# Local value products as four matmuls with a head's high and low parts side by side, and a slot's work in another order

## The chip, the cores and the metric

The kernel runs on one core of one Trainium2 chip. The metric is the device time of one execution in microseconds; the time before is the median of three runs. The engines are TensorE (PE in the profile, its weight loads PEld), VectorE (DVE), ScalarE (ACT), GpSimd (POOL) and SyncE (SP), whose queue starts the transfers.

## What is computed

Attention with a window and a few global tokens, for 8 batches of 8 heads, and behind it a feed-forward layer on all tokens. Sl is 512, Sg is 32, D is 64; the layer has d_model 512 and d_ff 2048. Cut to what matters:

```python
def _attn_ref(q_l, k_l, v_l, q_g, k_g, v_g):
    window, scale = 32, 1.0 / np.sqrt(D)
    k_all = np.concatenate([k_g, k_l], axis=2)
    v_all = np.concatenate([v_g, v_l], axis=2)
    out_g = sm(scale * q_g @ k_all.T) @ v_all            # global queries see all keys
    s_ll = np.where(np.abs(i - j) <= window, scale * q_l @ k_l.T, -1e9)
    s_lg = scale * q_l @ k_g.T                           # local queries: window and global keys
    out_l = sm(np.concatenate([s_lg, s_ll], -1)) @ np.concatenate([v_g, v_l], axis=2)
    return np.concatenate([out_g, out_l], axis=2)

def _moe_ref(x, w_in, w_out):
    h = np.maximum(x @ w_in, 0.0)
    return h * h @ w_out
```

## The kernel before

**Slots.** Batch, half of the sequence and head give 8 x 2 x 8 = 128 attention units of 256 queries. One loop runs over slots t. In slot t the scores and the softmax of unit t are computed, the probabilities of unit t-1 are transposed, split and multiplied by the values, and the inputs of unit t+1 are split. The same slot runs step m = t - 9 of the feed-forward layer: `gemm1` (two halves j of 12 products into `h`), `act1` and `act2` (relu, square, split into `gh` and `gl`), and `gemm2` of step m-1 (12 products into the two `o` tiles). Eight units make one group of 256 rows, and eight steps one block of the layer, so a block's output is copied out (`evac`, tile `ot`) every eighth slot, at t = 2 and 10 of 16. The global queries' own work is a list of jobs spread over slots; it repeats every 16 slots, which is one batch. Below, "slot 14" means t = 14 modulo 16.

**Split operands.** Units before t = 16 are plain: they use float32 products. From t = 16 on an operand is split in two parts of the type fp32r, a high part that is the rounded copy (made by ACT) and a low part that is the remainder (made by DVE, original minus high). A product is then high by high, high by low and low by high. `hi` holds a unit's keys (352 columns), queries (256) and values (256) in one tile, `lo` the remainders of the queries and of three quarters of the values; the keys' remainders lie in the lower 64 partitions of `hi`. `pt` (PSUM) holds the transposed probabilities, `ph` and `pl` their parts. `xa` (PSUM) is the attention output of a unit, transposed; `x_evac` splits it into `x_h` and `x_l`, the inputs of `gemm1`.

**Value products before.** `av` runs nine matmuls with weights of 64 columns (a value block, high or low) into the same 64 partitions of `xa`: for each half of the queries three with 128 columns, two more with 128 for the middle block, one with 256 for the global values, whose parts lie stacked.

**Buffers.** PSUM is full: two tiles `h`, two `o`, and one each of `pt`, `s`, `xa` and `gs`. The buffer of `xa` is shared with `gt` (the transposed global probabilities) and `gxo` (their products with the values), so each of these starts only when the last read of the one before is done. Global jobs that matter here, with their slots: `g_soft` and `g_exp` (2, 12), `g_norm` and `g_tr` with `gt` (3, 13), `g_rest` (`ptl`, `pth`) and the split of the first pair's values `gvh`, `gvl` (4, 14), `g_av` with `gxo` (4, 7, 14, 1), the split of the second pair's values (6, 0), `g_x` (5, 8, 15, 2).

**Order.** From t = 17 on every instruction of PE, DVE and ACT goes into its engine's queue in the order in which the program is written; `InOrder` sees to that, and it is why most lines of the profile carry the line of that helper (L52). Before that a scheduler chooses. A job's second number in the list is its place in the slot: 5 ahead of the scores, 4 ahead of the softmax, 3 behind it, 2 ahead of `gemm2`, 0 and 1 at the end.

Of the kernel before, what the change touches and what calls it, by code (L numbers as in the profile page):

```python
# [16 lines left out]
P = 128  # L17
# [9 lines left out]
LAG = 9  # L27
# [4 lines left out]
LOOK = 2  # L32
SQ = (2, 3, 4, 5, 14, 15)
MUL = 9
# [3 lines left out]
def f(ap):  # L38
    return ap.bitcast(F32)
# [19 lines left out]
def attention_moe(  # L59
# [22 lines left out]
    def plain(t):  # L82
        return t < NPLAIN
# [3 lines left out]
    def w_take(n):  # L87
        w_bufs["free"] -= n
# [35 lines left out]

    def split_head(t):

        hd = heads[t]
        raw = hd["raw"]
        if plain(t):
            return  # L130
        hi = p2.tile([P, PK], F32R, tag="hi", name=f"hi{t}")
        lo = p2.tile([P, QC + 192], F32R, tag="lo", name=f"lo{t}")
        ac.copy(hi, raw)
        ve.tensor_sub(lo, raw[:, KC : KC + QC + 192], f(hi[:, KC : KC + QC + 192]))
        ve.tensor_sub(hi[64:, :KC], raw[64:, :KC], f(hi[64:, :KC]))
        ve.tensor_sub(hi[32:64, PK - 64 :], raw[32:64, PK - 64 :], f(hi[32:64, PK - 64 :]))
        hd["hi"], hd["lo"] = hi, lo

# [45 lines left out]

    def softmax3(t):
        st = heads[t]["st"]
        pr = prob[t % 2]
        ve.tensor_scalar(out=st[:, 6:8], in0=st[:, 4:6], scalar1=1e-9, scalar2=None, op0=ALU.add)
        ve.reciprocal(out=st[:, 0:2], in_=st[:, 6:8])
        for u in range(2):  # L190
# [11 lines left out]
    def pt_split(t):  # L202
        hd = heads[t]
        if plain(t):
            pts = p2.tile([P, 512], F32, tag="gh", name=f"pts{t}")
            ac.copy(pts, pt)
            hd["pts"] = pts
            return
        ph = p1.tile([P, 640], F32R, tag="ph", name=f"ph{t}")
        pl = p1.tile([P, 256], F32R, tag="pl", name=f"pl{t}")  # L210
# [4 lines left out]
        hd["ph"], hd["pl"] = ph, pl  # L215

    def pt_rest(t):
        if plain(t):
            return
        ph, pl = heads[t]["ph"], heads[t]["pl"]  # L220
        ve.tensor_sub(pl, pt[:, :256], f(ph[:, :256]))
        ve.tensor_sub(ph[64:, 256:384], pt[:64, 320:448], f(ph[:64, 256:384]))

        ve.tensor_sub(ph[64:, 384:640], pt[64:, 256:512], f(ph[:64, 384:640]))

    def av(t):
        hd = heads[t]
        c = QC + KC
        if plain(t):

            xa = ps_a.tile([P, HALF], F32, tag="xa", name=f"xa{t}")
            v, pts = hd["raw"][:, c:], hd["pts"]
            mm = [
                (xa, v[:, 0:128], pts[:, 256:512]),
                (xa[:, 0:128], v[:, 64:192], pts[:, 0:128]),
                (xa[:, 128:256], v[:, 128:256], pts[:, 128:256]),
            ]
        else:
            xa = ps_a.tile([64, HALF], F32, tag="xa", name=f"xa{t}")
            vh, vl, ph, pl = hd["hi"][:, c:], hd["lo"][:, QC:], hd["ph"], hd["pl"]  # L240
            mm = []
            for u in range(2):
                o, vs, ps = xa[:, 128 * u : 128 * u + 128], slice(64 * u, 64 * u + 64), slice(128 * u, 128 * u + 128)
                mm += [(o, vh[:, vs], ph[:, ps]), (o, vl[:, vs], ph[:, ps]), (o, vh[:, vs], pl[:, ps])]
            o = xa[:, 64:192]
            mm += [(o, vh[:, 128:192], ph[:, 256:384]), (o, vl[:, 128:192], ph[:, 256:384])]
            mm.append((xa, vh[:, 192:256], ph[:, 384:640]))
        for i, (o, a, b) in enumerate(mm):
            pe.matmul(o, a, b, start=i == 0, stop=i == len(mm) - 1, skip_group_check=True)
        hd["xa"] = xa[:64, :]  # L250

    def x_evac(t):
        g, h = divmod(t, 8)
        xa = heads[t]["xa"]
        r = slice((h % 2) * 64, (h % 2) * 64 + 64)
        if g == 0:
            ac.copy(xg[r, h // 2, :], xa)
        else:
            ac.copy(x_h[r, g % 2, h // 2, :], xa)
            ve.tensor_sub(x_l[r, g % 2, h // 2, :], xa, f(x_h[r, g % 2, h // 2, :]))  # L260
        heads[t] = None
# [180 lines left out]

    def gemm1(m, j):
# [145 lines left out]
    for t in range(NSTEP + LAG + 1):  # L589
# [181 lines left out]
```

## Time and profile before

| | |
|---|---|
| median of the runs | 1068.83 us (1068.39 to 1069.07) |
| the profiled execution | 1068.82 us, span 1067.0 us |
| PE busy, matmuls | 1050.4 us (98%), 7568 |
| PEld busy | 941.7 us (88%) |
| DVE busy | 856.3 us (80%), 2687 instructions |
| ACT busy | 753.1 us (71%), 1901 instructions |
| granted TensorE clock | 1.00 |
| transfers | 96.78 MB, mean 91 GB/s |

Matmuls overlap, so PE's busy time is nearly the span and says little by itself. The chain of work that ended last tells more: followed back from the last instruction, it names at each step what released the next one. A group's line gives busy time and mean ns of one behind the bar, and behind a second bar the idle time of the engine just before it and what ended most of that. In the lines names stand without buffer numbers, output first: `xa<-ph,hi` is a product into xa.

### The profile page before, as it was taken

The page shows a single profiled execution, that of the slowest core. Times are in us where ns is not written, and L with a number is a line of the kernel's source. Part 1 is how long each engine was busy: PE and PEld are TensorE (multiplying, and loading weights), DVE is VectorE, ACT ScalarE, POOL GpSimd, SP SyncE. Part 2 cuts the span into 40 slices and gives each one's busy share as a digit, 9 for nine tenths or more (in the row PEclk, how much of TensorE's full clock was granted, in tenths as well). Part 3 has the DMA queues.
Part 4 walks back from the last instruction along what each step waited for, and adds up shares of the span by engine and source line. Part 5 has one row for each costly group of instructions (what it writes and reads, how often), then busy time and mean ns, then how long its engine had stood idle before and what let it go on. Part 6 is the DMA issues. An engine that isn't in the chain of part 4 may idle for free.

```text
span 1067.0 us, 21142 instructions
## 1 busy us (share of the span) xinstructions
PE 1050.4 (98%) x7568; PEld 941.7 (88%) x7568; DVE 856.3 (80%) x2687; ACT 753.1 (71%) x1901; POOL 3.9 (0%) x14
## 2 busy tenths in 40 slices
PE   7999999999999999999999999999999999999998
PEld 6776889999998989998999989999999989999896
DVE  5698988898888989988888888888888888874321
ACT  5898877778777776778777777777777787774322
POOL 1000000000000000000000000000000000000000
PEclk9999999999999999999999999999999999999999
DMA  9772132223222322222322222223221322201000
GB/s 372 310 263 74 57 106 76 71 80 98 68 89 64 103 65 83 74 91 77 94 71 82 86 72 76 90 66 100 78 89 55 94 86 66 88 29 33 13 20 20
DMA packets 54312, 96.78 MB, mean 91 GB/s; under 512 B 4288, under 2 KB 29376, under 8 KB 54208
## 3 DMA queue, kind: packets, MB, share of 16 engines
q1 hardware_dynamic: 54064, 95.37, 27.2%
q8 instruction: 60, 0.98, 0.4%
q14 instruction: 44, 0.36, 0.1%
q10 hardware_dynamic: 144, 0.07, 0.0%
HBM read 86.51 MB, written 8.91 MB: 89 GB/s over the span
## 4 chain that ended last, share of the span: by engine, by line
PE 87%; ACT 7%; DVE 4%; issue 1%; DMA 0%; ACTq 0%
PE o L52 33%; PE h L52 32%; PE xa L52 7%; PE s L52 6%; PE pt L52 5%; PE gxo L52 2%; PE gs L52 2%; ACT prob L52 1%; DVE prob L52 1%; ACT r L52 1%; ACT ph L52 1%; ACT hi L52 1%; ACT ot L52 1%; PE gt L52 1%; ACT sg L52 0%
## 5 line engine op out<-in xcount | busy, mean ns | idle before, releaser
L52 PE MATMUL h<-x_h,ws 128*128 128x256 f32 x2048 | 388.9, 283 | 0.0
L52 PEld LDWEIGHTS h<-x_h,ws 128*128 128x128 f32 x2048 | 327.0, 191 | 0.5
L52 PE MATMUL o<-ws,gh 128*128 128x512 f32 x1024 | 321.3, 395 | 0.0
L52 PE MATMUL h<-x_l,ws 128*128 128x256 f32 x1024 | 289.1, 282 | 0.1
L52 PEld LDWEIGHTS o<-ws,gh 128*128 128x128 f32 x1024 | 185.5, 188 | 34.6
L52 PE MATMUL o<-ws,gl 128*128 128x512 f32 x512 | 202.6, 396 | 0.0
L52 PEld LDWEIGHTS h<-x_l,ws 128*128 128x128 f32 x1024 | 195.9, 191 | 0.9 <-DVE x_l L52 0.4
L52 ACT CAST ph<-pt 128x256 fp32r<-128x256 f32 x448 | 141.1, 341 | 67.7 <-PE pt L52 60.8
L52 ACT ACTIVATE prob<-prob,st 128x224 f32<-128x224 f32 x270 | 127.8, 475 | 61.2 <-DVE st L52 59.1
L52 ACT ACTIVATE r<-h 128x512 f32<-128x512 f32 x136 | 81.4, 599 | 112.3 <-PE h L52 112.3
L52 PEld LDWEIGHTS o<-ws,gl 128*128 128x128 f32 x512 | 96.2, 188 | 22.7
L52 DVE CUSTOM_DVE_ANT_0 prob<-s,con 128x224 f32<-128x224 f32 x256 | 90.0, 386 | 24.5 <-PE s L52 23.2
L52 DVE TENSOR_TENSOR gl<-r,gh 128x512 fp32r<-128x512 f32 x128 | 87.9, 686 | 23.3 <-ACT gh L52 20.5
L52 ACT CAST hi<-raw 128x864 fp32r<-128x864 f32 x112 | 102.5, 915 | 1.4
L52 DVE TENSOR_TENSOR r<-h,r 128x512 f32<-128x512 f32 x82 | 56.7, 692 | 51.9 <-ACT r L52 50.6
L52 PE MATMUL xa<-ph,hi 128*64 128x128 f32 x448 | 87.3, 238 | 1.6 <-DVE ph L52 1.2
L52 DVE TENSOR_TENSOR hi<-raw,hi 64x352 fp32r<-64x352 f32 x224 | 82.5, 368 | 6.4
L52 ACT CAST gh<-r 128x512 fp32r<-128x512 f32 x128 | 79.1, 618 | 9.1 <-DVE r L52 8.7
L52 DVE TENSOR_TENSOR ph<-pt,ph 64x128 fp32r<-64x128 f32 x224 | 79.6, 355 | 7.0
L52 DVE TENSOR_TENSOR lo<-raw,hi 128x448 fp32r<-128x448 f32 x112 | 69.6, 622 | 15.3 <-ACT hi L52 12.5
L52 PE MATMUL pt<-con,prob 128*128 128x128 f32 (+1 forms) x512 | 78.2, 274 | 0.7 <-ACT prob L52 0.5
L52 DVE TENSOR_SCALAR prob<-prob,st 128x224 f32<-128x224 f32 x242 | 70.7, 334 | 4.1
(80 smaller groups left out, 1572.7 us busy)
## 6 DMA issues: line engine op xcount, KB each, us to landing
raw<-in_pk_dram SPq DMA_DIRECT2D x127, 432.0 KB, 3.2
wr<-in_w_dram SPq DMA_DIRECT2D x32, 512.0 KB, 7.9
gv<-in_vg_dram SPq DMA_DIRECT2D x32, 320.0 KB, 3.3
out_dram<-ot SPq DMA_DIRECT2D x32, 256.0 KB, 2.2
qr<-in_qg_dram SPq DMA_DIRECT2D x31, 64.0 KB, 2.8
out_dram<-ot SPq DMA_DIRECT2D x8, 64.0 KB, 1.7
con<-in_consts_dram SPq DMA_DIRECT2D x2, 224.0 KB, 5.1
raw<-in_pk_dram SPq DMA_DIRECT2D x1, 304.0 KB, 3.2
```

The source lines that it names most:

```text
L52: r = method(*args, **kwargs)
```

## The change

Four parts of one edit.

- **Values apart.** `split_head` becomes `split_kq` and `rest_kq` (keys and queries, tile `kq`, 608 columns copied by ACT, two remainders by DVE) and `split_v` (tile `v`, high and low part of each value block side by side in 128 columns). From t = 17 on `split_kq` and `rest_kq` of unit t+1 stand around the softmax of unit t; `split_v` stays late in the slot.
- **Four products.** The probabilities' parts lie side by side too (`ps`). A matmul has weights of 128 columns, the high and the low part of a value block, so `xa` has 128 partitions: high by high and high by low of the values come out one below the other, and the products with the low part of the probabilities in columns next to them. Four matmuls move 128, 256, 256 and 256 columns; the first two write their output in two pieces with a gap between. `x_evac` then adds up the parts: after the copy to `x_h` three operations on DVE that read `xa`, through a new tile `xr`, in place of one.
- **Order.** The remainders of the probabilities (`pt_rest`) go ahead of the softmax; `g_scores` and the value products go between the two halves of `gemm1`'s second part; `x_evac` goes ahead of `act1`; the scaling of the second half of the probabilities moves from DVE to ACT, behind the square.
- **Square.** It is on ACT in every slot up to t = 127, before in 6 of 16 slots (and on DVE in the others); behind that it is on DVE. The first output tile of a block takes the buffer of `pth` instead of one of its own. The host stacks the global values twice, 64 partitions apart, where it did three times, 32 apart.

```diff
-SQ = (2, 3, 4, 5, 14, 15)
...
+    def split_kq(t):
...
+        raw, c = hd["raw"], QC + KC
+        kq = p2.tile([P, c + QC], F32R, tag="kq", name=f"kq{t}")
+        ac.copy(kq[:, :c], raw[:, :c])
+        hd["hi"], hd["lo"] = kq[:, :c], kq[:, c:]
+
+    def rest_kq(t):
...
+        ve.tensor_sub(hd["lo"], raw[:, KC : KC + QC], f(hi[:, KC:]))
         ve.tensor_sub(hi[64:, :KC], raw[64:, :KC], f(hi[64:, :KC]))
-        ve.tensor_sub(hi[32:64, PK - 64 :], raw[32:64, PK - 64 :], f(hi[32:64, PK - 64 :]))
+
+    def split_v(t):
...
+        ac.copy(vs[:, :, :64], vr)
+        ve.tensor_sub(vs[:, :, 64:], vr, f(vs[:, :, :64]))
...
-            if MUL <= t < NPLAIN:
+            if MUL <= t < NPLAIN or t >= NPLAIN and u == 1:
                 ac.activation(out=w_, in_=w_, func=AF.Copy, scale=st[:, u : u + 1])
...
-        ac.copy(ph[:, :256], pt[:, :256])
-        ac.copy(ph[:64, 256:384], pt[:64, 320:448])
-        for r in (0, 32):
-            ac.copy(ph[r : r + 32, 384:640], pt[64:96, 256:512])
+        ac.copy(pb[:, :, 0, :], pt[:, :256].rearrange("p (u n) -> p u n", u=2))
+        ac.copy(ps[:64, 512:640], pt[:64, 320:448])
+        ac.copy(ps[:64, 640:], pt[64:, 256:])
...
+            xa = ps_a.tile([P, 512], F32, tag="xa", name=f"xa{t}")
+            xb = xa.rearrange("p (u h n) -> p u h n", u=2, h=2)
+            ps, vs = hd["ps"], [hd["v"][:, 128 * i : 128 * i + 128] for i in range(4)]
+            both = bass.AP(xa.tensor, xa.offset + 64, [list(xa.ap[0]), [192, 2], [1, 64]])
+            mm = [(both, vs[2], ps[:, 512:640]), (xb[:, :, 0, :], vs[3], ps[:, 640:])]
+            mm += [(xa[:, 256 * u : 256 * u + 256], vs[u], ps[:, 256 * u : 256 * u + 256]) for u in range(2)]
...
+            ac.copy(x0, xb[:64, :, 0, :])
+            ve.tensor_sub(xr, xb[:64, :, 0, :], f(x0))
+            ve.tensor_add(xr, xb[:64, :, 1, :], xr)
+            ve.tensor_add(x1, xb[64:, :, 0, :], xr)
...
-        if m < 8 or m + LAG < NT + 8 and (m + LAG) % 16 in SQ:
+        if m + LAG < NT:
             ac.activation(out=r, in_=r, func=AF.Square)
...
+        late, split = prev and not plain(t - 1), t + 1 < NT
         if prev:
             pt_split(t - 1)
+            if late:
+                pt_rest(t - 1)
...
+        if split and late:
+            split_kq(t + 1)
         if live:
             softmax1(t)
             softmax2(t)
-        if prev:
-            pt_rest(t - 1)
+        if split and late:
+            rest_kq(t + 1)
...
-            gemm1(m, 1)
+            gemm1(m, 1, 0 if late else None)
+        if live and not early:
+            g_scores(t)
         if prev:
             av(t - 1)
-        if live and not early:
-            g_scores(t)
+        if run and late:
+            gemm1(m, 1, 1)
...
         if live and not early:
-            softmax3(t)
+            softmax3(t, (0,))
+        if late:
+            x_evac(t - 1)
         if run:
             act1(m)
+        if live and not early:
+            softmax3(t, (1,))
```

How the queues read, on DVE in slot 14 before, from the softmax on: ISA and the row behind it are the masked maximum of one half of the scores `s`, `st` holds a row's maximum and sum, `prob` the probabilities; the rows with `gv` are the split of the global values.

```order
L52 ISA prob_93,st_2468<-s_2440,con 128x224
L52 ISA st_2468 128x1
...
L52 TENSOR_SCALAR st_2468<-st_2468 128x2
L52 TENSOR_TENSOR pl_2459<-pt,ph_2458 128x256
L52 TENSOR_TENSOR ph_2458<-pt,ph_2458 64x128
L52 TENSOR_TENSOR ph_2458<-pt,ph_2458 64x256
L52 TENSOR_TENSOR gvl_0_2478<-gv_0_2208,gvh_0_2477 128x512
L52 TENSOR_TENSOR gvh_0_2477<-gv_0_2208,gvh_0_2477 32x128
...
L52 RECIPROCAL st_2468<-st_2468 128x2
L52 TENSOR_SCALAR prob_93<-prob_93,st_2468 128x224 x2
L52 TENSOR_TENSOR x_l<-xa_2494,x_h 64x256
```

The probabilities' remainders stand behind the softmax, and one row reads xa.

The same slot on DVE now, from the remainders on (`ph` is the tile `ps` of the code):

```order
L51 TENSOR_TENSOR ph_2421<-pt,ph_2421 128x2x128
L51 TENSOR_TENSOR ph_2421<-pt,ph_2421 64x128
L51 TENSOR_TENSOR ph_2421<-pt,ph_2421 64x256
L51 TENSOR_TENSOR ptl_2428<-gt_2389,pth_2394 128x512
...
L51 ISA prob_93,st_2434<-s_2403,con 128x224
...
L51 TENSOR_TENSOR kq_2432<-raw_2290,kq_2432 128x256
...
L51 TENSOR_TENSOR gvl_0_2443<-gv_0_2177,gvh_0_2442 128x512
...
L51 TENSOR_SCALAR prob_93<-prob_93,st_2434 128x224
L51 TENSOR_TENSOR xr_2469<-xa_2455,x_h 64x256
L51 TENSOR_TENSOR xr_2469<-xa_2455,xr_2469 64x256
L51 TENSOR_TENSOR x_l<-xa_2455,xr_2469 64x256
```

The remainders stand ahead of the softmax, those of k and q between it and the global values, and three rows read xa.

On ACT in the same slot before, from the copies of `pt` on:

```order
L52 CAST ph_2458<-pt 32x256 x2
L52 CAST pth_2431<-gs_2290 64x128
L52 ACTIVATE prob_93,st_2468<-prob_93,st_2468 128x224 x2
L52 CAST gvh_0_2477<-gv_0_2208 128x640
L52 ACTIVATE r_2510<-h_2445 128x512
L52 ACTIVATE r_2510<-r_2510 128x512
L52 CAST x_h<-xa_2494 64x256
L52 CAST hi_2515<-raw_2324 128x864
L52 CAST gh_2535<-r_2510 128x512
```

And on ACT now:

```order
L51 CAST ph_2421<-pt 64x256
L51 CAST pth_2394<-gs_2245 64x128
L51 CAST kq_2432<-raw_2290 128x608
L51 ACTIVATE prob_93,st_2434<-prob_93,st_2434 128x224 x2
L51 CAST gvh_0_2442<-gv_0_2177 128x640
L51 CAST x_h<-xa_2455 64x256
L51 ACTIVATE r_2474<-h_2408 128x512
L51 ACTIVATE r_2474<-r_2474 128x512
L51 ACTIVATE prob_93<-prob_93,st_2434 128x224
L51 CAST v_2478<-raw_2290 128x4x64
L51 CAST gh_2495<-r_2474 128x512
```

The copy of keys and queries stands ahead of the exponentials (the row with x2), the copy of the values late; x_h has moved ahead of r, and a scaling of prob stands behind the square.

On PE around the value products, before:

```order
L52 MATMUL h_2445<-x_h,ws_994 128x256
L52 MATMUL xa_2494<-ph_2458,hi_2301 64x128
L52 MATMUL xa_2494<-ph_2458,lo_2302 64x128
L52 MATMUL xa_2494<-pl_2459,hi_2301 64x128
...
L52 MATMUL xa_2494<-ph_2458,hi_2301 64x256
L52 MATMUL gs_2504<-hi_2400,qgz 128x288
L52 MATMUL o_2_2105<-ws_961,gh_2422 128x512 x2
```

And now:

```order
L51 MATMUL h_2408<-x_h,ws_992 128x256
L51 MATMUL gs_2453<-kq_2321,qgz 128x288
L51 MATMUL xa_2455<-ph_2421,v_2270 128x2x64
L51 MATMUL xa_2455<-ph_2421,v_2270 128x2x128
L51 MATMUL xa_2455<-ph_2421,v_2270 128x256 x2
L51 MATMUL h_2408<-x_h,ws_995 128x256
```

Four products stand where nine stood, behind gs, and six of h behind them.

More of the change, by code (lines that the diff above doesn't have):

```diff
@@ L123, in attention_moe @@
     nc.vector.memset(pt[96:, 256:], 0.0)
-    def split_head(t):
-        hd = heads[t]
-        raw = hd["raw"]
+    def split_kq(t):
         if plain(t):
             return
[L131 to L134, printed above, removed]
-        ve.tensor_sub(hi[64:, :KC], raw[64:, :KC], f(hi[64:, :KC]))
-        ve.tensor_sub(hi[32:64, PK - 64 :], raw[32:64, PK - 64 :], f(hi[32:64, PK - 64 :]))
-        hd["hi"], hd["lo"] = hi, lo
+        hd = heads[t]
+        raw, c = hd["raw"], QC + KC
[3 more added lines that the diff above has]
+    def rest_kq(t):
+        if plain(t):
+            return
+        hd = heads[t]
+        raw, hi = hd["raw"], hd["hi"]
+        ve.tensor_sub(hd["lo"], raw[:, KC : KC + QC], f(hi[:, KC:]))
+        ve.tensor_sub(hi[64:, :KC], raw[64:, :KC], f(hi[64:, :KC]))
+    def split_v(t):
+        if plain(t):
+            return
+        hd = heads[t]
+        vt = p2.tile([P, 2 * VC], F32R, tag="v", name=f"v{t}")
+        vr = hd["raw"][:, QC + KC :].rearrange("p (b n) -> p b n", b=4)
+        vs = vt.rearrange("p (b n) -> p b n", b=4)
+        ac.copy(vs[:, :, :64], vr)
+        ve.tensor_sub(vs[:, :, 64:], vr, f(vs[:, :, :64]))
+        hd["v"] = vt
     def scores(t):
@@ L183, in softmax2, with softmax3 @@
             )
-    def softmax3(t):
+    def softmax3(t, tiles=(0, 1)):
         st = heads[t]["st"]
         pr = prob[t % 2]
-        ve.tensor_scalar(out=st[:, 6:8], in0=st[:, 4:6], scalar1=1e-9, scalar2=None, op0=ALU.add)
-        ve.reciprocal(out=st[:, 0:2], in_=st[:, 6:8])
-        for u in range(2):
+        if 0 in tiles:
+            ve.tensor_scalar(out=st[:, 6:8], in0=st[:, 4:6], scalar1=1e-9, scalar2=None, op0=ALU.add)
+            ve.reciprocal(out=st[:, 0:2], in_=st[:, 6:8])
+        for u in tiles:
             w_ = pr[:, WIN * u : WIN * (u + 1)]
-            if MUL <= t < NPLAIN:
+            if MUL <= t < NPLAIN or t >= NPLAIN and u == 1:
                 ac.activation(out=w_, in_=w_, func=AF.Copy, scale=st[:, u : u + 1])
@@ L238, in av @@
         else:
[L239 to L247, printed above, removed]
+            xa = ps_a.tile([P, 512], F32, tag="xa", name=f"xa{t}")
[4 more added lines that the diff above has]
+            mm += [(xa[:, 256 * u : 256 * u + 256], vs[u], ps[:, 256 * u : 256 * u + 256]) for u in range(2)]
         for i, (o, a, b) in enumerate(mm):
             pe.matmul(o, a, b, start=i == 0, stop=i == len(mm) - 1, skip_group_check=True)
-        hd["xa"] = xa[:64, :]
+        hd["xa"] = xa
     def x_evac(t):
@@ L256, in x_evac @@
         if g == 0:
-            ac.copy(xg[r, h // 2, :], xa)
-        else:
-            ac.copy(x_h[r, g % 2, h // 2, :], xa)
-            ve.tensor_sub(x_l[r, g % 2, h // 2, :], xa, f(x_h[r, g % 2, h // 2, :]))
+            ac.copy(xg[r, h // 2, :], xa[:64, :])
+            heads[t] = None
+            return
+        x0, x1 = x_h[r, g % 2, h // 2, :], x_l[r, g % 2, h // 2, :]
+        if plain(t):
+            ac.copy(x0, xa[:64, :])
+            ve.tensor_sub(x1, xa[:64, :], f(x0))
+        else:
+            xb = xa.rearrange("p (u h n) -> p u h n", u=2, h=2)
+            x0, x1 = [x.rearrange("p (u n) -> p u n", u=2) for x in (x0, x1)]
+            xr = p1.tile([P, 2, P], F32, tag="xr", name=f"xr{t}")[r]
+            ac.copy(x0, xb[:64, :, 0, :])
+            ve.tensor_sub(xr, xb[:64, :, 0, :], f(x0))
+            ve.tensor_add(xr, xb[:64, :, 1, :], xr)
+            ve.tensor_add(x1, xb[64:, :, 0, :], xr)
         heads[t] = None
@@ L456, in gemm1 @@
         for n, (a, b) in enumerate(mm):
-            pe.matmul(hp[:, j, :], a, b, start=n == 0, stop=n == len(mm) - 1)
+            if half in (None, 2 * n // len(mm)):
+                pe.matmul(hp[:, j, :], a, b, start=n == 0, stop=n == len(mm) - 1)
     def act1(m):
@@ L504, in evac @@
         for i in tiles:
-            pool, tag = ((p1, "ot"), (p2, "gl"))[i]
+            pool, tag = ((p1, "pth"), (p2, "gl"))[i]
             ot = pool.tile([P, DM], F32, tag=tag, name=f"ot{blk}_{i}")
@@ L632, in attention_moe @@
         if live and not early:
-            softmax3(t)
+            softmax3(t, (0,))
+        if late:
+            x_evac(t - 1)
         if run:
             act1(m)
-        if prev:
+        if live and not early:
+            softmax3(t, (1,))
+        if prev and not late:
             x_evac(t - 1)
-            if plain(t - 1):
-                w_take(-1)
+            w_take(-1)
         if early:
@@ L642, in attention_moe @@
         w_tick(t, 1)
-        if t + 1 < NT:
-            split_head(t + 1)
+        if split and not late:
+            split_kq(t + 1)
+            rest_kq(t + 1)
+        if split:
+            split_v(t + 1)
         if live:
@@ L729 @@
             pk[:, hf, :, 64 * dup : 64 * dup + 64, c + 128 : c + 192] = vw[:, :, 128:192]
-        for dup in range(3):
-            pk[:, hf, :, 32 * dup : 32 * dup + 32, c + 192 : c + 256] = v_g
+        for dup in range(2):
+            pk[:, hf, :, 64 * dup : 64 * dup + 32, c + 192 : c + 256] = v_g
     pk = pk.reshape(NT, P, PK)
```

16 lines of the change are left out of this document (8 added, 8 removed).

## The prediction

> **What bounds the kernel now.** I read the page first, for the busy shares and the chain that ended last, then the same numbers for one block of 16 slots, then the chain and the timeline of single slots.
>
> ```profile
> PE 1050.4 (98%) x7568; PEld 941.7 (88%) x7568; DVE 856.3 (80%) x2687; ACT 753.1 (71%) x1901; POOL 3.9 (0%) x14
> PE 87%; ACT 7%; DVE 4%; issue 1%; DMA 0%; ACTq 0%
> 378.68:500.94 122.26, 121.89 (x928) 111.51 (x928) 106.76 (x341) 90.72 (x235) 0.00 (x0) 1.00 0.26 81
> ```
>
> The third line is a table by stretch: length, then PE, PEld, DVE, ACT and POOL busy, then the granted clock (1.00). These 16 slots repeat seven times. PE is idle for 0.37 us of 122.26, DVE for 15.5, ACT for 31.5. So PE's queue sets the pace, and DVE is next. The profiled execution took 1068.82 us (span 1067.0 and 1.8 around it), the median of the runs is 1068.83, so the sum below is made on 1068.8.
>
> The chain of one ordinary slot and the start of the next (start, length, what):
>
> ```profile
> 394.40 2.88 PE h L52 x24
> 397.28 0.59 PE xa L52 x9
> 397.88 0.13 PE gs L52
> 398.01 2.79 PE o L52 x12
> 400.80 0.44 PE pt L52 x4
> 401.24 0.44 PE s L52 x4
> ```
>
> These lines add up to 7.27 us, and nothing but PE stands in them. In such a slot a matmul saved is time saved, and a new wait on PE is time lost. Not all slots are like that. This is slot 14 of 16, where the global heads' probabilities and values are split as well (start, length, engine, operation; in brackets the idle time before and who ended it):
>
> ```profile
> 452.82 0.60 PE L52 MATMUL pt<-con,prob 128*128 128x128 f32 x4
> 453.51 1.30 ACT L52 CAST ph<-pt 128x256 fp32r<-128x256 f32 x4
> 453.64 0.69 DVE L52 TENSOR_TENSOR ptl<-gt,pth 128x512 fp32r<-128x512 f32 x1
> 455.12 0.29 DVE L52 TENSOR_TENSOR pth<-gs,pth 64x128 fp32r<-64x128 f32 x1 [0.80 <-ACT pth L52]
> 455.43 0.39 DVE L52 CUSTOM_DVE_ANT_0 prob<-s,con 128x224 f32<-128x224 f32 x1
> 456.25 0.42 DVE L52 TENSOR_TENSOR pl<-pt,ph 128x256 fp32r<-128x256 f32 x1
> 456.38 0.48 ACT L52 ACTIVATE prob<-prob,st 128x224 f32<-128x224 f32 x1 [1.29 <-DVE st L52]
> 456.70 0.74 DVE L52 TENSOR_TENSOR ph<-pt,ph 64x128 fp32r<-64x128 f32 x2
> 457.21 0.22 PE L52 MATMUL xa<-ph,lo 128*64 128x128 f32 x1
> 457.33 0.71 ACT L52 CAST gvh<-gv 128x640 fp32r<-128x640 f32 x1
> 457.73 0.29 PE L52 MATMUL gs<-hi,qgz 128*128 128x288 f32 x1
> 458.07 0.69 DVE L52 TENSOR_TENSOR gvl<-gv,gvh 128x512 fp32r<-128x512 f32 x1 [0.62 <-ACT gvh L52]
> 459.09 0.17 DVE L52 TENSOR_SCALAR st<-st 128x2 f32<-128x2 f32 x1
> 459.49 0.58 DVE L52 TENSOR_SCALAR prob<-prob,st 128x224 f32<-128x224 f32 x2
> 460.11 0.42 DVE L52 TENSOR_TENSOR x_l<-xa,x_h 64x256 fp32r<-64x256 f32 x1
> 460.65 0.22 PE L52 MATMUL gxo<-gvh,pth 128*64 128x128 f32 x1
> 461.43 0.62 PE L52 MATMUL pt<-con,prob 128*128 128x128 f32 x4
> ```
>
> gxo shares its PSUM buffer with xa, so it can start only after DVE's last read of xa. That read ends at 460.53 and gxo starts at 460.65: no slack is left here before the change. The waits say the same for all gxo:
>
> ```profile
> PEld gxo L52 <- DVE x_l L52: 3.3, 14, 0.8
> ```
>
> **The change, part by part.** *PE.* Nine products (0.59) become four. Three of them move 256 columns, like h, 2.88/24 = 0.12 each. The fourth moves 128 columns through weights 128 wide. Nothing before is just that: the eight narrow ones cost (0.59-0.12)/8 = 0.06 each, with weights 64 wide; the pt transposes, 128 or 96 wide, 0.44/4 = 0.11. The second is nearer. So 0.42 to 0.47, I take 0.45: 0.14 saved per slot, 2.2 in 16.
>
> *ACT and DVE.* Durations by rows (mean ns behind the bar):
>
> ```profile
> L52 ACT CAST hi<-raw 128x864 fp32r<-128x864 f32 x112 | 102.5, 915 | 1.4
> L52 ACT CAST ph<-pt 32x256 fp32r<-32x256 f32 x224 | 82.0, 366 | 4.1
> L52 ACT ACTIVATE r<-r 128x512 f32<-128x512 f32 x54 | 34.1, 632 | 1.6
> L52 ACT ACTIVATE prob<-prob,st 128x224 f32<-128x224 f32 x270 | 127.8, 475 | 61.2 <-DVE st L52 59.1
> L52 DVE TENSOR_TENSOR r<-h,r 128x512 f32<-128x512 f32 x82 | 56.7, 692 | 51.9 <-ACT r L52 50.6
> L52 DVE TENSOR_TENSOR lo<-raw,hi 128x448 fp32r<-128x448 f32 x112 | 69.6, 622 | 15.3 <-ACT hi L52 12.5
> L52 DVE TENSOR_TENSOR x_l<-xa,x_h 64x256 fp32r<-64x256 f32 x120 | 49.6, 414 | 14.8 <-ACT x_h L52 12.9
> L52 DVE TENSOR_TENSOR pl<-pt,ph 128x256 fp32r<-128x256 f32 x112 | 47.1, 421 | 2.8 <-ACT ph L52 1.9
> L52 DVE TENSOR_TENSOR hi<-raw,hi 32x64 fp32r<-32x64 f32 x112 | 24.1, 215 | 3.2
> ```
>
> ACT in 16 slots: one of the two 366 ns copies goes (-5.9); hi of 864 columns becomes 608 and 256: between the 128x640 copy (0.71) and the 864 one, about 0.70, plus about 0.40, so 1.10 for 0.915 (+3.0); ten squares come over from DVE (+6.3); one scaling of prob comes over, at most the 475 of this row (+7.6). That is +11, 102 of some 120: not the bound by its sum. DVE: ten squares go (-6.9), the 32x64 goes (-3.4), lo shrinks from 448 to 256 columns (622 to the 421 of pl, -3.2), one of two scalings goes (0.58 becomes about 0.33, -4); the values' remainder comes (+6.7) and two more operations on xa (2 x 414, +13.2). That is +2.4, 109 of 120, beside 6 us of gaps that no wait explains. By sums all of it still fits below PE, so what decides is who waits for whom.
>
> *The order in a slot.* DVE now makes the remainders of the probabilities (pl and two ph: 456.25 to 457.44, 1.2 us) ahead of the softmax, not behind it. So in every slot the exponentials on ACT start 1.2 us later, and behind them in ACT's queue stand x_h, r, the square and the second scaling of prob, for which PE's next transposes wait. In an ordinary slot counted from its first transpose: ph copied at 0.6, remainders from 1.0 to 2.2, exponentials 3.2 to 4.2, x_h 4.6, r 5.2 (taken as long as the square), square 5.85, prob 6.35, and the transposes come at 7.13. That hides. The early split of k and q hides too: ACT does its 0.70 while DVE makes the remainders, DVE its two (about 0.42 and 0.52) while ACT runs the exponentials; without that cover they would put 0.9 on prob, 0.2 more than the margin of 7.13 - 6.35. No transfer is moved past another in SP's queue, and a load still has a slot's time ahead of its use. The first output tile of a block now lies in pth's buffer; pth is next written a slot later, and an output lands in 2.2 us:
>
> ```profile
> out_dram<-ot SPq DMA_DIRECT2D x32, 256.0 KB, 2.2
> ```
>
>
> *Slots 4 and 14.* Here it doesn't hide. From ph's start: first copy 0.40, remainders 1.22, ptl 0.72, pth 0.31, softmax to the exponentials 0.95 (455.43 to 456.38), exponentials 0.95 (to 457.33), gvh 0.74 (to 458.07), gvl and gvh's remainder 1.02 (to 459.09), sum and reciprocal 0.40, one scaling 0.36, and the three operations on xa 1.31: 8.4 us, where before it was 453.51 to 460.53, 7.0. ph starts 0.7 after the first transpose, so xa is free at 9.1 and gxo starts at 9.2. PE without waits would be there at 7.35 (460.65 - 452.82 = 7.83, less 0.14, and less a wait of 0.34 for ph that this slot had: 457.21 to 457.73 is 0.52, of which 0.06 and 0.12 are the last two products). PE waits 1.85, gxo takes 0.78, and the slot takes 10.0 for the 8.61 before (452.82 to 461.43): +1.4. With each link 0.03 off, 1.1 to 1.7.
>
> *Slots 3 and 13* end with gt, which uses xa's buffer too:
>
> ```profile
> 450.70 0.41 DVE L52 TENSOR_TENSOR x_l<-xa,x_h 64x256 fp32r<-64x256 f32 x1
> 452.38 0.60 PE L52 MATMUL gt<-con,sg 128*128 128x128 f32 x4
> ```
>
> The margin was 1.3. The chain grows by the early k and q remainders (about 1.0) and two operations on xa (0.9), less the square (0.7) and a scaling (0.25): 1.0. Then up to 1.0 more if the slot starts late because ACT's longer queue ends with the global exponentials. So 0 to 0.9 lost, I take 0.4, between the ends.
>
> *Slots 2 and 10* copy two output tiles on ACT between the exponentials and x_h:
>
> ```profile
> 487.30 1.07 ACT L52 COPY ot<-o 128x512 f32<-128x512 f32 x2
> ```
>
> 6.35 + 1.07 = 7.4 against transposes at 7.13: 0.25 (0 to 0.5). *Slots 1 and 7* follow slots in which DVE ends late with another gvl, and the values' products now stand 0.9 us earlier on PE (0.72 of h and 0.13 of gs): 0.25 (0 to 0.5) waiting for the remainders. What goes: 16 slots take 122.26 where PE's own work is 16 x 7.27, four gxo of 0.78 and some 1.2 of transposes, 120.6. Of these 1.7 us of waits, the ones in slots 4 and 14 are counted above; of the other 1.0 I take 0.6 as gone with the early split of k and q (0 to 1.0).
>
> *The sum for 16 slots:* 14 x -0.14 = -2.0; +2.8; +0.8; +0.5; +0.5; -0.6: +2.0. Times seven: +14 us. Head and tail change little (the tail squares on DVE, which is idle there). 1068.8 + 14 = 1083. With all ends low, -2.4 + 2.2 - 1.0 = -1.2, or 1060; with all ends high, -1.7 + 3.4 + 1.8 + 1.0 + 1.0 = +5.5, or 1107.
>
> **Rivals.** *The work stays covered and the saving shows.* If DVE's chain in slots 4 and 14 is 1.0 us shorter than I laid it (the point at which these slots cost only 0.4) and the small waits don't come, then 16 slots give -2.0 + 0.8 - 0.6, and the time is about 1056. For it: DVE's 15 idle us per block. Against it: ACT and DVE alternate in that chain, each link waits for the other engine, so idle time elsewhere doesn't shorten it, and its margin is zero already. *The products themselves are slow.* Two of the four write PSUM in two pieces with a gap; no matmul before does. If such a write doubled their time, 0.06 to 0.11 and 0.12 more per slot, the saving is gone and 112 x 0.2 = 22 us come on top of the forecast: 1105. Nothing in the rows speaks for it. The Trainium skill, PSUM — Partial Sum Buffer, Specifications, says that any non-contiguous access pattern slows matmuls significantly, beside cachelines of 8 bytes; no run here shows that yet. The pieces are 64 and 128 columns long, so I give it little. That wider weights eat the saving is excluded: h loads the same 128 columns at 0.12. *Cancelling.* Loss and saving meet within 0.2%, 1066.7 to 1071, about what a measurement of this kernel can tell from no change.
>
> **Numbers.** Forecast 0.62, covered 0.22, cancelling 0.09, slow products 0.07. So faster 0.22, same 0.09, slower 0.69. The range for 8 in 10 goes from 1060, the low ends, to 1100; the forecast's own is 1072 to 1100.
>
> **What would show it.** Right: xa's group with x448 and about 0.45 per slot in the chain; DVE x_l ahead of gxo with some 1.5 us of wait in slots 4 and 14, so some 20 us for gxo in the waits; these slots near 10.0, ordinary ones near 7.13; PE idle above 4 us per block. Wrong: gxo's wait below 0.5, or ordinary slots above 7.27, which would be the products or ACT's second scaling.

## The result, and the profile after

| | median of 3 runs | range | span of the profiled execution |
|---|---|---|---|
| before | 1068.83 us | 1068.39 to 1069.07 | 1067.0 us |
| changed | 1130.37 us | 1130.27 to 1130.56 | 1128.5 us |

The changed kernel takes 1.0577 times as long (95% interval 1.0560 to 1.0595), 61.5 us more. The forecast was 1083, its range ended at 1100.

The page after: the busy shares, and the shares of the chain that ended last.

```profile
PE 1053.4 (93%) x7008; PEld 926.7 (82%) x7008; DVE 880.7 (78%) x2734; ACT 795.8 (71%) x2078; POOL 3.9 (0%) x14
ACT 38%; DVE 33%; PE 20%; issue 6%; DMA 1%; SPq 0%; DVEq 0%; ACTq 0%
```

DVE is busy 24 us more and ACT 43 us more, both still far below the span. For a block of 16 slots that is 3.0 on DVE (forecast 2.4) and 6.6 on ACT (forecast at most 11). But PE's share of the chain fell from 87% to 20%, and ACT and DVE now hold 71% of it. The kernel has a new bound that no busy share shows: the two engines waiting for each other. One block of 16 slots, in the columns of the prediction's third line:

```profile
397.88:528.56 130.68, 122.34 (x849) 109.35 (x848) 109.78 (x347) 97.33 (x261) 0.00 (x0) 1.00 0.25 75
```

PE stood still for 8.3 us of a block, before for 0.37; the granted clock is the same 1.00. The waits by engine (us in total, times, longest):

```profile
ACT prob L51 <- DVE st L51: 203.5, 123, 4.4
DVE ph L51 <- ACT ph L51: 56.6, 78, 1.5
PE gxo L51 <- DVE x_l L51: 22.3, 15, 2.1
PE o L51 <- ACT ot L51: 15.1, 14, 1.2
PE gs L51 <- DVE pth L51: 9.6, 15, 0.9
PE gt L51 <- DVE x_l L51: 7.1, 14, 1.3
PE xa L51 <- DVE ph L51: 5.7, 32, 0.5
```

The first row is in the main the exponentials waiting for the softmax's maxima; before, that wait was 59.1. The next is new. The five of PE are where the time is lost.

The slots' lengths, first transpose of one slot to that of the next, read from the timelines; beside them when the exponentials start, counted from the slot's first transpose (us):

```
slot                 4    5    6    7    8    9   10   11   12   13   14   15    0    1    2    3
length before     8.62 7.36 7.33 8.05 7.30 7.29 7.27 7.27 7.27 7.73 8.61 7.39 7.32 8.05 7.28 8.12
length after     10.72 7.17 7.15 8.73 7.17 7.15 8.65 7.14 7.42 8.71 10.55 7.18 7.40 8.83 8.38 8.33
exponentials bef. 3.55 2.12 2.45 2.72 2.05 2.05 2.02 2.02 2.20 2.05 3.56 2.15 2.81 2.80 2.05 2.44
exponentials aft. 4.96 3.77 3.95 4.73 3.92 3.81 4.04 3.75 4.30 4.53 4.80 3.78 4.30 4.83 3.78 4.15
```

Ordinary slots are shorter, as forecast (7.14 to 7.18; forecast 7.13). Nearly all the loss sits in eight of 16 slots: 4, 14, 2, 10, 1, 7, 3 and 13. A block grew from 122.28 to 130.68, by 8.4 us; the 108 slots from t = 20 to 127 grew by 56.7, what stands ahead of them by 4.2 (3.9 of it in t = 17 to 19, the first three slots in program order) and the tail by 0.6, together the 61.5 of the two spans.

**Slot 14**, the one shown before (timeline after; in brackets the idle time and who ended it):

```profile
478.57 0.91 ACT L51 CAST ph<-pt 128x256 fp32r<-128x256 f32 x3
479.51 1.16 DVE L51 TENSOR_TENSOR ph<-pt,ph 128x256 fp32r<-128x256 f32 x3 [0.79 <-ACT ph L51]
480.69 0.69 DVE L51 TENSOR_TENSOR ptl<-gt,pth 128x512 fp32r<-128x512 f32 x1
481.41 0.29 DVE L51 TENSOR_TENSOR pth<-gs,pth 64x128 fp32r<-64x128 f32 x1
481.76 0.40 PE L51 MATMUL gs<-kq,qgz 128*128 128x288 f32 x1 [0.58 <-DVE pth L51]
...
487.07 0.43 DVE L51 TENSOR_TENSOR x_l<-xa,xr 64x256 fp32r<-64x256 f32 x1
487.65 0.24 PE L51 MATMUL gxo<-gvh,pth 128*64 128x128 f32 x1 [1.52 <-DVE x_l L51]
```

From the start of ph to the end of x_l is 8.93 us; forecast 8.4. Two things are to be seen. DVE's first remainder starts at 479.51, behind the end of all three copies of ACT (478.57 + 0.91), not behind the first: half a microsecond. And gs, which the change put ahead of the value products, waits 0.58 for pth, since the sequence of DVE with pth in it now begins with the remainders.

**Slot 10**, the output tiles:

```profile
450.01 0.48 ACT L51 ACTIVATE prob<-prob,st 128x224 f32<-128x224 f32 x1 [1.59 <-DVE st L51]
451.07 1.07 ACT L51 COPY ot<-o 128x512 f32<-128x512 f32 x2
451.71 0.73 PE L51 MATMUL o<-ws,gh 128*128 128x512 f32 x2 [1.23 <-ACT ot L51]
```

The copies stand behind the exponentials on ACT, and the first product of the next block writes the tile that they read. With the exponentials late, o waits 1.23 us.

**Slot 7**, the remainders late:

```profile
425.49 1.18 DVE L51 TENSOR_TENSOR ph<-pt,ph 128x256 fp32r<-128x256 f32 x3
425.96 0.29 PE L51 MATMUL gs<-kq,qgz 128*128 128x288 f32 x1
426.36 0.30 PE L51 MATMUL xa<-ph,v 128*128 128x128 f32 x1
426.81 0.59 PE L51 MATMUL xa<-ph,v 128*128 128x256 f32 x3 [0.16 <-DVE ph L51]
```

gs takes 0.13, the first product of xa 0.06, so without waits these two rows of xa would start at 426.09 and 426.15. They start at 426.36 and 426.81: 0.66 lost.

**An ordinary slot** (the chain; start, length, what), from one slot's ph to the next one's:

```profile
455.25 0.53 ACT ph L51 x2
455.80 0.38 ACT ph L51
456.20 0.42 DVE ph L51
...
458.16 0.18 DVE st L51
458.37 0.81 ACT prob L51 x3
459.43 0.37 ACT x_h L51
...
460.96 0.37 ACT prob L51
461.33 0.30 ACT v L51
461.65 0.42 ACT sg L51 x2
462.10 0.30 ACT qgz L51
462.40 0.52 ACT gh L51
462.95 0.37 ACT ph L51
```

No PE in it. The loop from ph to ph takes 7.70 us here; PE needs 7.14 for the slot. The scaling of prob is done at 461.33, in time for PE's transposes, so this slot itself loses nothing. But ACT still has v, sg, qgz and gh ahead of the next ph, and so the next slot starts with ACT later: ph begins 0.63 us after the first transpose in slot 11, 1.19 in slot 12 and 1.43 in slot 13, and slot 13 then stalls: its value products lose 0.5 us to the late remainders, and gt waits another 0.46 for x_l. In the other ordinary slots the loop takes 7.0 to 7.7 us.

### The profile page after: what moved, and what is told of

Its sections match the earlier page's. It is cut to its first block, busy times and chain, and to the rows that moved or that the text cites. A ratio compares the mean times of both kernels' runs of the same rounds, so it can differ in the third digit from the quotient of the medians.

```text
span 1128.5 us, 20154 instructions
## 1 busy us (share of the span) xinstructions
PE 1053.4 (93%) x7008; PEld 926.7 (82%) x7008; DVE 880.7 (78%) x2734; ACT 795.8 (71%) x2078; POOL 3.9 (0%) x14
## 4 chain that ended last, share of the span: by engine, by line
ACT 38%; DVE 33%; PE 20%; issue 6%; DMA 1%; SPq 0%; DVEq 0%; ACTq 0%
DVE ph L51 11%; ACT prob L51 9%; PE o L51 8%; DVE prob L51 8%; ACT r L51 7%; ACT ph L51 7%; PE h L51 6%; DVE st L51 3%; ACT gh L51 3%; ACT sg L51 3%; ACT x_h L51 2%; DVE xr L51 2%; PE gxo L51 2%; ACT v L51 2%; DVE gvl L51 2%
## 5 line engine op out<-in xcount | busy, mean ns | idle before, releaser
L51 PE MATMUL h<-x_h,ws 128*128 128x256 f32 x2048 | 406.5, 283 | 0.0
L51 ACT ACTIVATE prob<-prob,st 128x224 f32<-128x224 f32 x382 | 180.2, 473 | 203.7 <-DVE st L51 203.5
L51 DVE TENSOR_TENSOR ph<-pt,ph 128x256 fp32r<-128x256 f32 x336 | 127.2, 379 | 62.4 <-ACT ph L51 56.6
L51 DVE TENSOR_TENSOR kq<-raw,kq 128x256 fp32r<-128x256 f32 x224 | 106.1, 474 | 1.7 <-ACT kq L51 0.2
L51 ACT CAST ph<-pt 128x256 fp32r<-128x256 f32 x336 | 99.9, 332 | 6.8 <-PE pt L51 1.7
L51 DVE CUSTOM_DVE_ANT_0 prob<-s,con 128x224 f32<-128x224 f32 x256 | 90.6, 389 | 17.4 <-PE s L51 13.3
L51 PE MATMUL xa<-ph,v 128*128 128x128 f32 x448 | 79.9, 286 | 7.5 <-DVE ph L51 5.7
L51 ACT CAST kq<-raw 128x608 fp32r<-128x608 f32 x112 | 78.2, 699 | 3.6 <-DMA raw<-in_pk_dram 3.6
L51 ACT ACTIVATE r<-r 128x512 f32<-128x512 f32 x119 | 75.2, 632 | 3.7
L51 PEld LDWEIGHTS xa<-ph,v 128*128 128x128 f32 x448 | 64.1, 189 | 15.9 <-issue 14.8
L51 PE MATMUL s<-kq 128*128 128x224 f32 x448 | 76.8, 293 | 0.0
```

The costliest lines, as they stand in the source:

```text
L51: r = method(*args, **kwargs)
```

## The experiments

Theory A is that the order does it: remainders ahead of the softmax, and what comes late behind them. The rivals put it on the new layout's own work, or on one wait alone. Times are medians, ratios are against the kernel before, which ran beside them (1068.55 to 1068.81).

**The remainders back behind the softmax**, ahead of the remainders of k and q; all else as changed.

```diff
-            if late:
-                pt_rest(t - 1)
...
             softmax2(t)
+        if late:
+            pt_rest(t - 1)
```

> The changed kernel, only with the remainders of the probabilities put back behind the softmax. Theory A (the order costs: the exponentials start 1.8 us later in each slot, which delays the output copies, gs, and the split of the global values): the waits of o for ot and of gs for pth go, gxo's shrinks to about 0.4, so about 6.8 us per 16 slots less than the changed kernel, 1080 to 1090. Theory B (the layout costs: two more DVE operations on xa in each slot, which don't fit): the waits only move to other places, 1115 or more.

Measured: 1087.14 us, ratio 1.0168 (1.0151 to 1.0185).

```profile
ACT prob L51 <- DVE st L51: 36.8, 60, 4.4
PE xa L51 <- DVE ph L51: 12.7, 46, 0.9
```

This is inside theory A's 1080 to 1090. One move takes back 43.2 of the 61.5 us, and the wait in the first row falls from 203.5 to 36.8. Of what a block gets back, 2.6 us lie in slots 4 and 14, 2.7 in slots 2 and 10 (o hardly waits for ot now), 1.1 in slot 13 and 0.3 in slots 1 and 7; slots 0 and 6 lose 0.4. What is new is the longer wait of the value products for the remainders, which are late for products that stand 0.9 us earlier on PE.

**The output tiles copied ahead of the softmax**, and no more behind the exponentials.

```diff
+        if 0 < m <= NSTEP and m % 8 == 1 and m > 8:
+            evac(m // 8 - 1)
         if live:
             softmax1(t)
```

> The changed kernel, only with the two copies of o to ot put ahead of the softmax in ACT's queue, where ACT waits for DVE anyway. Theory A: the wait of o for ot, 1.2 us twice in 16 slots, and what x_h and r lose behind it go: about 2.8 us per 16 slots, so 1110 to 1113. Theory B: these slots are held by DVE's chain anyway, and less than 8 us are won, 1122 or more.

Measured: 1114.30 us, 1.0425 (1.0409 to 1.0441). That is 1.3 us above theory A's 1113. The wait of o for ot is gone, and 16.1 us with it. Slots 2 and 10 fall to 7.2, by 1.2 and 1.5, more than they had grown (1.10 and 1.38); slot 3 grows by 0.4. The first experiment takes the same 2.7 out of slots 2 and 10, so the gains of the two runs don't add up.

**The layout alone, in the old order**: late split of k and q, remainders behind the softmax, scalings and squares where they were, the value products behind all of h and ahead of gs.

```diff
+SQ = (2, 3, 4, 5, 14, 15)
...
-            if MUL <= t < NPLAIN or t >= NPLAIN and u == 1:
+            if MUL <= t < NPLAIN:
...
-        if split and late:
-            split_kq(t + 1)
...
-            gemm1(m, 1, 0 if late else None)
-        if live and not early:
-            g_scores(t)
+            gemm1(m, 1)
         if prev:
             av(t - 1)
+        if live and not early:
+            g_scores(t)
```

> Only the four products with their layout, in the order of the kernel before: k, q and values split late, remainders behind the softmax, both scalings and ten of 16 squares on DVE, value products behind all of h. DVE then has 106.8 + 13.9 = 121 us per 16 slots of work and 6 of gaps. Theory A: PE's saving of 2.2 shows except where this sum is over PE's 120, so about 127 per block at most: 1070 to 1100. Theory B: 1100 or more, with DVE over 95% busy.

Measured: 1121.72 us, 1.0494 (1.0478 to 1.0509).

```profile
PE 1058.1 (95%) x7008; PEld 928.9 (83%) x7008; DVE 942.2 (84%) x2911; ACT 722.3 (65%) x1901; POOL 4.5 (0%) x14
PE s L52 <- DVE kq L52: 13.3, 27, 1.6
PEld s L52 <- ACT ph L52: 20.6, 21, 1.2
```

Neither theory held: the time is theory B's, but DVE is not over 95% busy (84% of the span, 118.3 of 129 us in a block). The order of the change was not the whole of the loss. The layout gives DVE 86 us more than before (856.3), and in the old order the scores wait, for the remainders of k and q on DVE in the second row, for ACT in the third (where the profile names a copy to ph). So some parts of the change's order must be earning what others lose; the next runs look for which.

**The same, with squares and one scaling on ACT**, the scaling directly behind the exponentials; the diff is against the kernel above.

```diff
-SQ = (2, 3, 4, 5, 14, 15)
...
-            if MUL <= t < NPLAIN:
+            if MUL <= t < NPLAIN or t >= NPLAIN and u == 1:
...
-        if m < 8 or m + LAG < NT + 8 and (m + LAG) % 16 in SQ:
+        if m + LAG < NT:
```

> As the run before (four products in the old order), but with every square up to slot 127 and the scaling of the second half of the probabilities on ACT, as in the changed kernel. DVE has 109 us per 16 slots. Theory A: close to PE's own 118.4 per block, waits only at gxo in two of 16 slots (0.3 to 0.6 us each): 1045 to 1062, faster than before. Theory B: the three operations on xa hold gxo and gt here too, 1090 or more.

Measured: 1241.98 us, 1.1619 (1.1602 to 1.1636), a plain miss.

```profile
ACT prob L51 <- DVE st L51: 293.0, 227, 4.4
DVE xr L51 <- ACT x_h L51: 210.1, 111, 2.9
```

ACT's scaling waits for the sum and the reciprocal on DVE, and x_h is queued behind it. DVE waits for x_h. The granted clock was 0.98 in this run and 1.00 in the run above, a difference of 2% beside 11% of time.

**The global values split a slot earlier**, so that gvl and gvh are out of the chain of slots 4 and 14.

```diff
-                (d + 3, 3, g_split_v, 0),
+                (d + 2, 2, g_split_v, 0),
```

> The changed kernel, only with the split of the first global pair's values (gvh on ACT, gvl and gvh's remainder on DVE) moved from the middle of slots 4 and 14 to the end of slots 3 and 13. Theory A (a chain ACT, DVE, ACT, DVE in slots 4 and 14 holds gxo): the chain loses 0.74 and 1.02, gxo's wait of 1.5 goes, and up to 0.5 of it comes back because slots 4 and 14 start later on ACT: 2 to 3 us per 16 slots less, 1109 to 1116. Theory C (DVE has no room left in these slots, so the same work is only paid elsewhere): within 5 us of the changed kernel.

Measured: 1115.82 us, 1.0438 (1.0421 to 1.0456). This is inside theory A's 1109 to 1116, at its slow end. gxo waits no more, and slots 14 and 4 take 9.42 and 9.71 instead of 10.55 and 10.72, but not the 7.9 that they would need without waits (7.13 and gxo's 0.78):

```profile
PE gs L51 <- DVE pth L51: 17.4, 14, 1.7
```

gs's wait for pth was 9.6 and is now 17.4: the second wait in these slots, that the prediction had not seen, comes forward.

**Remainders behind the softmax, and the value products behind all of h** (ahead of them gemm1's second half whole; on ACT part 0 of `act1`, the copy r of h, ahead of x_h, and part 1, the square, behind it). This stands on top of the first experiment's edit.

```diff
-            gemm1(m, 1, 0 if late else None)
+            gemm1(m, 1)
...
-        if run and late:
-            gemm1(m, 1, 1)
...
+        if run:
+            act1(m, 0)
         if late:
             x_evac(t - 1)
         if run:
-            act1(m)
+            act1(m, 1)
```

> As the first run (remainders behind the softmax), and the value products back behind all of h, with relu ahead of the copy to x_h on ACT. Theory A: the first run's waits of xa for the remainders (0.4 to 0.65 us in some six of 16 slots) go, 18 us; the three operations on xa start 0.4 later, which gxo feels in two slots, 5 us: 1070 to 1076. Theory C (DVE has no room): gxo and gt take what xa gives back, 1084 or more.

Measured: 1069.21 us, 1.0006 (0.9997 to 1.0016), no difference from the kernel before, and just under theory A's 1070. The parts of the order that are taken back here account for 61.2 of the 61.5 us: 43.2 and another 17.9.

**The same with the global values split early**, with the edit of `g_split_v` shown above.

> As the run before it, and with the global split moved to the end of slots 3 and 13 as well. Theory A: what is left of gxo's waits goes, so 10 to 14 us less than that run, 1058 to 1064, faster than the kernel before. Theory C: 1072 or more.

Measured: **1065.48 us, 0.9970 (0.9959 to 0.9981)**, 0.3% faster than the kernel before, a small difference but clear of the noise. Theory A had asked for more: 10 to 14 us less than the run above, where 3.7 came. A block, and the chain of one ordinary slot in it:

```profile
402.42:523.62 121.20, 119.75 (x847) 109.23 (x846) 109.29 (x347) 96.25 (x261) 0.00 (x0) 1.00 0.26 81
424.81 0.44 PE pt L51 x4
425.25 0.44 PE s L51 x4
425.69 2.87 PE h L51 x24
428.56 0.13 PE gs L51
428.69 0.46 PE xa L51 x4
429.16 2.80 PE o L51 x12
```

Only PE stands in the slot, and it takes 7.14 to 7.17. In the span the slots from t = 20 to 127 are together 6.8 us shorter than before; what stands ahead of them costs 3.7 more, nearly all in t = 17 to 19. Slots 4, 14 and 3 are still longer than before (9.18, 8.83 and 8.24).

**The third copy of the probabilities in a tile of its own**, all else as changed.

```diff
+        pg = p1.tile([P, 256], F32R, tag="pg", name=f"pg{t}")
...
-        ac.copy(ps[:64, 640:], pt[64:, 256:])
+        ac.copy(pg[:64, :], pt[64:, 256:])
```

> The changed kernel, only with the global columns of the probabilities (the third copy of pt and its remainder) in a tile of their own. It asks why DVE's first remainder starts behind ACT's third copy and not behind the first, 0.57 us later than forecast. If it waits because both write one tile, it starts 0.5 earlier in every slot and the time falls by 15 to 30 us, to 1100 to 1115. If it waits because ACT still reads pt, the start stays at the end of the third copy, and the time at 1128 to 1132.

Measured: 1130.5 us in one run.

```profile
DVE ph L51 <- ACT pg L51: 56.8, 78, 1.5
```

The wait is the same 56.8 us in 78 places, now on the copy into pg. So it isn't the tile that is written. One reading left is that ACT still reads pt, of which DVE's first remainder reads the same partitions. Another is the signal: DVE waits on a semaphore (the counter by which one engine tells another that it is done), and in all 112 slots the trace records no update of it by ACT's first copy, so DVE had nothing to start on at that copy's end. No run took this apart.

**Three global jobs moved later**, on the best version: the split of the global probabilities (`g_rest`) behind the softmax, `g_soft` and `g_norm` behind the operations on xa. gs goes behind the value products too (`g_scores` behind `av`, not shown).

```diff
-                (d + 1, 3, g_soft),
+                (d + 1, 2, g_soft),
...
-                (d + 2, 3, g_norm),
+                (d + 2, 2, g_norm),
...
-                (d + 3, 4, g_rest),
+                (d + 3, 3, g_rest),
```

> The run with remainders behind the softmax, products behind h and the global split early, and now three global jobs out of the way as well: the split of the global probabilities (ptl, pth) behind the local remainders, the maxima and the reciprocals of the global softmax (g_soft, g_norm) behind the operations on xa, and gs behind the value products. Theory A: in that run 16 slots still lose 0.8 (slot 14), 1.1 (slot 4) and 0.65 (slot 3) to waits of xa, gxo and gt; most of this goes: 1048 to 1054, and the whole saving of 15.7 us that the products promise shows. Theory C (DVE has no room): 1062 or more.

Measured: 1089.10 us, 1.0195 (1.0181 to 1.0209), a miss.

```profile
PE xa L51 <- DVE ptl L51: 28.0, 14, 2.7
```

Slot 14 takes 11.6 and 10.1 in turn, slot 4 10.6. ptl is the last read of gt, and gt lies in the buffer of xa: the value products cannot write until it is done, and I had moved it behind the softmax.

**The same with ptl back in its place**, and only the remainder of pth (a part of its own, `g_rest2`) behind the softmax; the diff is against the kernel above.

```diff
-                (d + 3, 3, g_rest),
+                (d + 3, 4, g_rest),
+                (d + 3, 3, g_rest2),
```

> As the run with the global jobs behind xa, but ptl stays ahead of the softmax: it is the last reader of gt, which lies in xa's buffer, so the value products of slots 4 and 14 waited 1.8 us and more for it there. Only pth's remainder moves behind the local remainders. Theory A: ordinary slots 7.15, slots 4 and 14 some 8.3, slot 3 8.0, so 119.6 us per 16 slots for the 121.2 of the run without these moves: 1050 to 1058, faster than the kernel before by 1 to 1.7%. Theory C (DVE has no room): the waits appear at another place, 1062 or more.

Measured: 1083.90 us, 1.0147 (1.0130 to 1.0164), a miss again. Slots 14 and 4 take 9.87 and 10.42 (twice 11.97). By the timeline DVE enters them late, because `g_norm` and gvl now both stand at the end of slots 3 and 13, and the value products and gs wait for it:

```profile
PE xa L51 <- DVE ph L51: 11.4, 36, 1.2
PE gs L51 <- DVE pth L51: 9.5, 13, 0.7
```

**k and q split late again**, on the version that equals the kernel before.

```diff
-        if split and late:
-            split_kq(t + 1)
...
-        if split and late:
-            rest_kq(t + 1)
...
-        if split and not late:
+        if split:
```

> The run with remainders behind the softmax and products behind h, only with keys and queries split late in the slot again, as before the change. Theory A: DVE stands idle while ACT runs the exponentials, and the scores of the next slot wait for the keys' remainders: 0.3 to 1.0 us in each slot, 1100 to 1150. If the early split is worth nothing: 1069 to 1075.

Measured: 1089.73 us, 1.0198 (1.0184 to 1.0212), 20.5 us slower. The early split is worth that; I had expected more.

**The scaling on ACT ahead of the square**, on that version too.

```diff
-            softmax3(t, (0,))
+            softmax3(t)
...
-            act1(m)
-        if live and not early:
-            softmax3(t, (1,))
+            act1(m, 1)
```

> The run with remainders behind the softmax and products behind h, only with ACT's scaling of the second half of the probabilities ahead of relu and the square, behind the exponentials. Theory A: it waits for DVE's reciprocals, and relu, the copy to x_h and the square stand behind it in ACT's queue, some 1 us in each slot; the operations on xa start that much later: 1085 to 1110 or more. If its place doesn't matter: 1069 to 1075.

Measured: 1175.43 us, 1.0999 (1.0984 to 1.1014), 106 us slower.

```profile
ACT prob L51 <- DVE st L51: 248.3, 197, 4.4
DVE xr L51 <- ACT x_h L51: 128.6, 112, 1.8
```

These are the two waits of the 1242 us run, which was 120 us slower than the other kernel in the old order; so the place of the scaling can account for most of that. One scaling of 0.47 us on ACT, put ahead of r, x_h and the square, holds up all of these until DVE has the sum.

## Why the prediction was wrong

The sign and the mechanism at slots 4 and 14 were right, the size was not: 61.5 us for a forecast of 14. Nearly all the signs that the prediction had named for its own account came, x_l ahead of gxo with 1.5 us of wait and PE idle above 4 us in a block among them; they tested the mechanism and not the size. The rivals by which the time falls or stays are out, with PE idle for 8.3 us in a block. Term by term, for 16 slots (us; a forecast of "+0.4" stood beside the saving of 0.14 in the same slot, which is taken off here):

| slots | forecast | measured |
|---|---|---|
| the other eight | -1.1 | -0.75 |
| 4 and 14 | +2.8 | +4.04 |
| 3 and 13 | +0.5 | +1.19 |
| 2 and 10 | +0.2 | +2.48 |
| 1 and 7 | +0.2 | +1.46 |
| waits regained | -0.6 | some -0.2 in slots 5, 6 and 15, in the first row |
| sum | +2.0 | +8.4 |

- **The products** were sized right. Nine of 0.59 became four of 0.46, forecast 0.45, and PE's busy time in a block fell by 2.1 in the best version (119.75 for 121.89), forecast 2.2. The rival of slow products is out: two of the four write PSUM in pieces with a gap, and with nothing else in the way a slot is 7.15.
- **The durations of the added operations** were right too: the copy of k and q 0.70 for 0.70, that of the values 0.39 for 0.40, the operations on xa 0.41 to 0.43 for 0.414. The first of these in the groups (busy time and mean ns behind the bar):

```profile
L51 ACT CAST kq<-raw 128x608 fp32r<-128x608 f32 x112 | 78.2, 699 | 3.6 <-DMA raw<-in_pk_dram 3.6
```

- **"The exponentials on ACT start 1.2 us later."** They start 1.7 later (3.75 for 2.02 in slot 11). The step that failed is "first copy 0.40, remainders 1.22": I let DVE start behind ACT's first copy of pt, and it starts behind the third. This is 0.5 in every slot, and nearly all of what was missing in the chain of slots 4 and 14 (8.93 for 8.4).
- **"That hides."** This is the step that failed in most of the other slots. For the ordinary slot I followed the chain to the scaling of prob and compared it with PE's next transposes, 6.35 against 7.13. Measured, that holds even so: slot 11 took 7.14. But the late exponentials have more behind them than that. In slots 2 and 10 these are the copies of the output tiles (next point). In every slot ACT's queue goes on through v and gh, in some through sg and qgz, to the next ph, and the loop from ph to ph, 7.70 in the slot shown, has to fit into 7.14 on the average of the slots. Where it doesn't, the lag grows from slot to slot until one stalls. That the place of the remainders is the main cause is shown: taking them out of the loop removed 43.2 us, and from slot 11 to 12 ph then follows ph after 7.24. How much of this is the lag and how much the lateness within one slot was not tried apart; by the timelines, the lag is behind the 1.1 us of slot 13, while slots 2, 10, 4 and 14, which got back 5.3 us, had ph at most 0.25 us later than before and lost by the lateness within the slot.
- **Slots 2 and 10** were the biggest miss for one place. I looked at what the late copies of the output tiles do to prob (0.25), not at who waits for the copied tile: the next block's first product, 1.2 us. With the copies moved ahead, 16.1 us went; with the remainders moved back, these slots lost the same.
- **Slots 4 and 14.** Each grew by 2.0, forecast 1.4. gxo waits 1.5 us for x_l (forecast 1.85), and gs 0.6 to 0.7 for pth ahead of it, which I hadn't counted: the change sets gs ahead of the value products and pth behind three remainders. The early split of the global values takes the wait of gxo away, and gs's grows in its place.
- **Slots 1, 7, 3 and 13.** Slots 1 and 7 had the right cause and too small a price: in slot 7 it was 0.66 of waiting for the remainders, where I said 0 to 0.5. In slot 3 gt waits 0.45 for x_l, as forecast (0.4). In slot 13 that is only half: the other 0.5 is xa waiting for the remainders, which the lag that came with "That hides" has made late and which I had priced in slots 1 and 7 alone.
- **"Head and tail change little."** The tail does change little (0.6 us). What stands ahead of t = 20 cost 4.2 us, which I had at nothing; the best version has 3.7 of them still. In t = 17 to 19 the trace shows waits of the same kinds (gxo 0.54, o for ot 0.93, xa 0.46, gt 1.28). It also shows one that the prediction had ruled out with "a load still has a slot's time ahead of its use": at t = 18 to 20 ACT's early copy of k and q waits for its load, 3.6 us in three places (in the row above). No run tells these apart.
- **The diff's parts, by the runs:** the early split of k and q is worth 20.5 us and the scaling behind the square 106 us, both on the version with the other two parts taken back. The remainders ahead of the softmax and the products between the halves of h cost 61.2 together. The second edit also puts r ahead of x_h on ACT; which of its two halves counts was not tried apart. The move of the squares to ACT was not tried alone either.

## What to carry to other kernels

With engines that work through their queues in order, follow a chain not to the first reader that is in time but around to the same instruction of the next step: what counts is the loop's length against the pace of the bounding engine, and an excess of half a microsecond shows up several steps later and somewhere else. When an instruction becomes late, list what stands behind it in its queue, and for each of these who waits for it, buffers that it reads included: here a copy of an output tile was the dearest that the forecast had missed. An edit that saves work on the bounding engine should come with the old order of the others wherever they had no slack; here the same four products with two parts of the order taken back and one global job moved gave 1065.48 instead of 1130.37.

## What the runs showed of the hardware

- **Matmuls into PSUM in two pieces cost at most a few hundredths of a microsecond here**, with pieces of 64 and 128 columns: four products took 0.46 us, where the prediction's sum by plain rows was 0.42 to 0.47. The Trainium skill, PSUM — Partial Sum Buffer, Specifications, says that any non-contiguous pattern slows matmuls significantly; for pieces of this length these runs don't agree.
- **ACT and DVE did not read one PSUM tile at the same time** in any of the 14 traces. In the changed kernel DVE's first remainder waited for the end of ACT's third copy in 78 places, 56.6 us in all, and as long with the third copy in another SBUF tile. The Trainium skill, PSUM — Partial Sum Buffer, PSUM bank collisions raise a hardware error, says that the compiler sets a dependency between two engines' accesses to the same bank and 32 partitions, reads too. The wait agrees with that: pt is one buffer, the remainder reads all 128 partitions, the third copy the upper 64. That this is the cause stays argued; putting the columns into two buffers was not tried.
- **A scaling of 0.47 us in the wrong place of a queue cost 106 us**, or 0.95 on the average of the 111 slots from t = 17 on, from nothing in some slots to 2.8 in slot 13.
